# Weight slots of 4096 bytes, with the first two bytes of each row's piece left out of the load

## The chip, the core and the metric

The kernel runs on one core of one Trainium2 chip. The metric is the device time of one execution in microseconds; a kernel's time is the median over its runs.

## The reference

Pooled attention, whose output goes through a channel mix. Keys and values are averaged over 8 neighbouring positions, so that each of 576 queries sees 72 keys; the channel mix blends each token with the one before it, and then has a squared-ReLU layer and a sigmoid gate.

```python
# q, k, v: (8, 8, 576, 64)
k_p = k.reshape(B, H, Sp, pool, D).mean(axis=3)
v_p = v.reshape(B, H, Sp, pool, D).mean(axis=3)
scores = scale * np.matmul(q, k_p.transpose(0, 1, 3, 2))
attn = softmax(scores)
x = np.matmul(attn, v_p)            # then to (8, 576, 512)
# x_prev is x one token earlier
xk = mu_k * x + (1.0 - mu_k) * x_prev
xr = mu_r * x + (1.0 - mu_r) * x_prev
k = np.maximum(xk @ w_k, 0.0)       # w_k 512 x 1024
v = k * k @ w_v                     # w_v 1024 x 512
r = 1.0 / (1.0 + np.exp(-(xr @ w_r)))   # w_r 512 x 512
return r * v
```

The three weight arrays are float64, 10.5 MB together.

## The kernel before

The 4608 tokens are worked off in 12 chunks of 384. For each chunk the kernel computes scores, softmax, the attended values (`attended`), the blend with the token before (`shifted`), the hidden layer (`hidden`, matmuls at L1125), the gate (`gate`, L1178) and the output (`mixed`, L1211). The chunks from the second on multiply operands that are split into a high and a low part, three matmuls for one product; the first chunk (chunk 0) multiplies whole float32 operands.

The weights lie in HBM as float64, in 20 pieces of 128 rows by 512 doubles: `wk0` to `wk7`, `wr0` to `wr3`, `wv0` to `wv7`. A load (L589) moves one piece: 4096 bytes of each of 128 rows, 512 KB. A piece becomes float32 on the chip in `convert`: one cast (L621 on ScalarE, L624 on GpSimd or L627 on VectorE, by the table `TOP_BY`) takes the top two bytes of each double as a bf16 and writes them as the upper half of a float32 word in a scratch tile (its name in the profile is `turned`), and VectorE's L630 shifts the four bytes below them by 13 bits and joins the two. L630 writes over the front half of the same slot. `split` (L645 or L648, L656) later makes the high and low parts.

The lowest two bytes of a double take no part in this. The load before puts a row's 4096 bytes at byte 2 of its slot, so that the four bytes that L630 reads begin at a multiple of four:

```python
words = got[:, 1:2 * WP + 1].rearrange("p (n two) -> p n two", two=2)[:, :, 0]
first = got.bitcast(BF16)[:, 2:4 * WP + 2].rearrange("p (n four) -> p n four", four=4)[:, :, 2]
```

That leaves the slot 4224 bytes long (1056 int32), of which the last 126 are empty.

The order of the instructions of each engine is worked out by the program itself when it is built (class `Order`, with the table of due times `DUE`); each engine, and SyncE which issues nearly all DMAs (SPq in the profile), works its list off in that order. SyncE's first loads are written out by hand: "k0 k1 q1 wk1 q0 wk0 r0 q5 v0 q2 v1 wr2 v2 wr3 wk7 k2 q4 wv4 c0 wv6 q3 k3 wk3 wv1 wv2 wk5 wk2 wv7 wv3 v3 wr1 wr0 wk4 wv5 r1 wv0 wk6". A letter alone stands for keys, values, the values of the last keys, queries or constants (in the profile `in_kT`, `in_vm`, `in_vr`, `in_qT`, `in_mask` and `in_mu`). Some of these land in tiles that are used for something else later on: `early_sl`, `early_xrl`, `turned`. `summed` (L671) adds up keys and values over 8 positions with matmuls against an identity.

Of the kernel before, what the change touches and what calls it, by code (L numbers as in the profile page):

```python
# [10 lines left out]
I32 = mybir.dt.int32  # L11
BF16 = mybir.dt.bfloat16
F16 = mybir.dt.float16
U16 = mybir.dt.uint16
# [5 lines left out]
P = 128  # L20
# [11 lines left out]
WP = 512  # L32
# [315 lines left out]
def dve(n, lock=True):  # L348
    return "dve", 0.067 + n / 960, lock
# [15 lines left out]
def attention_then_channel_mix(  # L365
# [20 lines left out]
    sb = ctx.enter_context(tc.tile_pool(name="sb", bufs=1))  # L386
# [63 lines left out]
    for tag, n in (("sl", 2), ("xrl", 1), ("turned", 2)):  # L450
# [4 lines left out]
        for i in range(n):  # L455
            got = t[:, i]
# [93 lines left out]
    sources = {"k": w_k, "r": w_r, "v": w_v}  # L550
    held = {}

    def loads():

        for what in LOADS.split():
            kind, i = what[:-1] if what[0] == "w" else what[0], int(what.lstrip("ckvrqw"))
            yield from load(kind, i)
        done = set(LOADS.split())
        for i in range(NT):
            for b, s, *_ in tiles[i][2]:  # L560
                if first_tile[b] == i:
                    for what in (f"k{2 * b}", f"k{2 * b + 1}", f"v{2 * b}", f"v{2 * b + 1}", f"r{b}"):
                        if what not in done:
                            yield from load(what[0], int(what[1:]))
            if f"q{i}" not in done:
                yield from load("q", i)

    def load(kind, i):
        if kind == "c":
            yield "sp", 1.0, False  # L570
            nc.sync.dma_start(out=mask_sb, in_=mask)
            nc.sync.dma_start(out=mu_sb, in_=mu)
            order.fetched("mask", 100)
            order.fetched("mu", 100)
            return
        if kind == "q":
            qs = yield take("qs")
            yield "sp", 0.6, False
            nc.sync.dma_start(out=qs, in_=qT[i])
            held["q", i] = qs  # L580
            order.fetched(("q", i), 262)
            return
        if kind[0] == "w":
            slot = yield take("w")
            yield "sp", 0.6, False
            got = sb.tile([P, 2 * WP + 32], I32, name=f"got_{kind}{i}", tag=f"w{slot}")
            held["got", kind[1], i] = got
            held["slot", kind[1], i] = slot
            nc.sync.dma_start(  # L589
                out=got.bitcast(U16)[:, 1:1 + 4 * WP],  # L590
                in_=sources[kind[1]][:, i * WP:(i + 1) * WP].bitcast(U16),
            )
            order.fetched((kind, i), 512)
            return
        src, rows, cols = {
            "k": lambda: (kT[i // 2, :, 2 * (i % 2):2 * (i % 2) + 2, :], P, KEYS),
            "v": lambda: (vm[i // 2, :, 2 * (i % 2):2 * (i % 2) + 2, :], P, D),
            "r": lambda: (vr[i], 4 * KR, D),
        }[kind]()
        st = yield take("stage")  # L600
        yield "sp", 0.6, False
        v = st[:rows, :2 * POOL * cols].rearrange("p (g n) -> p g n", g=2)
        nc.sync.dma_start(out=v, in_=src)  # L603
        held[kind, i] = st, v
        order.fetched((kind, i), 2 * POOL * cols * rows / 256)

    def convert(kind, i):

        yield need(("w" + kind, i))
        got = held.pop(("got", kind, i))
        words = got[:, 1:2 * WP + 1].rearrange("p (n two) -> p n two", two=2)[:, :, 0]
        first = got.bitcast(BF16)[:, 2:4 * WP + 2].rearrange("p (n four) -> p n four", four=4)[:, :, 2]
        top = yield take("tmp")
        upper = top.bitcast(F16).rearrange("p (n two) -> p n two", two=2)[:, :, 1]
        by = TOP_BY[kind][i]
        if by == "a":
            yield "act", 0.62, False  # L620
            nc.scalar.copy(out=upper, in_=first)  # L621
        elif by == "g":
            yield "pool", 0.91, True
            nc.gpsimd.tensor_copy(out=upper, in_=first)  # L624
        else:
            yield "dve", 0.42, True
            nc.vector.tensor_copy(out=upper, in_=first)  # L627
        yield dve(WP)
        full[kind, i] = got[:, :WP].bitcast(F32)
        nc.vector.scalar_tensor_tensor(  # L630
            out=got[:, :WP], in0=words, scalar=13, in1=top.bitcast(I32),
            op0=ALU.logical_shift_right, op1=ALU.bitwise_or,
        )
        order.give("tmp", top)
        order.make(("full", kind, i))
# [605 lines left out]
    for b in range(B):  # L1241
        i = first_tile[b]
# [5 lines left out]
    for kind, n in (("k", NJT), ("r", NCT), ("v", NJT)):  # L1248
        for i in range(n):
            at = {"k": FIRST + 2.6 * i - 4, "r": FIRST + 20 + 2 * i - 3, "v": FIRST + 28 + 2.5 * i}[kind]  # L1250
            order.add(at, convert(kind, i))
            used = []
            if whole(0, kind):
                used = [("hid", 0, i, p) for p in range(len(PARTS))] if kind == "k" else [("gated" if kind == "r" else "mixed", 0)]
            at = {"k": 2.1 * i - 4, "r": 15 + i, "v": 25 + 0.8 * i}[kind]
            if not used:
                order.add({"k": FIRST + 2.6 * i - 3.5, "r": FIRST + 20 + 2 * i - 2.5, "v": FIRST + 28.5 + 2.5 * i}[kind], split(kind, i))
            else:
                order.add(later + at, split(kind, i, *used))
    for i in range(NT):  # L1260
# [11 lines left out]
        n = REST_BY[min(c, len(REST_BY) - 1)]  # L1272
# [73 lines left out]
```

## Time and profile before

| | |
|---|---|
| median of 3 runs | 600.98 us (600.29 to 601.49) |
| the profiled execution | 599.92 us |
| its span in the trace | 598.1 us |
| TensorE (PE) busy | 587.9 us, 98% of the span |
| VectorE (DVE) busy | 360.6 us, 60% |
| ScalarE (ACT) busy | 319.5 us, 53% |
| GpSimd (POOL) busy | 206.0 us, 34% |
| weight loads | 20, of 512 KB each, issued from 2.1 to 37.3 us |
| median us from issue to landing | wk 8.7, wr 9.3, wv 9.9 |

The profiled execution lasts 1.8 us longer than its span. A time from issue to landing holds the time that a load stands in the queues behind earlier ones, so it is long where many loads are in flight. The chain of waits in the profile goes back from the last instruction to what released it, and is what decides the time; busy time of an engine outside of it costs nothing.

### The profile page before, as it was taken

How to read it: one execution, taken by the hardware profiler on the slowest of the kernel's cores; microseconds unless marked ns; L12 is line 12 of the kernel's file. 1: busy time of each engine (PE TensorE's matmuls, PEld its weight loads, DVE VectorE, ACT ScalarE, POOL GpSimd, SP SyncE). 2: the span in 40 equal slices, each digit the busy share in tenths (PEclk: the TensorE clock that was granted, in tenths of full speed). 3: DMA queues.
4: the chain of work that ended last, by engine and by line, in shares of the span. 5: the costliest groups of instructions: out<-in, count | busy, mean ns of one | idle time of the engine just before them, and what ended most of it. 6: DMA issues, size and time to landing. Idle time of an engine off the chain costs nothing.

```text
span 598.1 us, 10517 instructions
## 1 busy us (share of the span) xinstructions
PE 587.9 (98%) x4026; PEld 491.4 (82%) x4026; DVE 360.6 (60%) x743; ACT 319.5 (53%) x657; POOL 206.0 (34%) x291
## 2 busy tenths in 40 slices
PE   7899999999999999999999999999999999999997
PEld 6766457978978988978978988987988988978985
DVE  5889978956967727657836726673954424423411
ACT  3577867657566463675555445555565335343420
POOL 1133276365126337147115309118416006005000
PEclk9999999999999999999999999999999999999999
DMA  8995075165364135335423115424014000001001
GB/s 322 405 380 188 39 191 172 43 173 204 115 179 114 45 80 175 121 104 151 168 57 77 59 37 157 133 93 115 19 61 94 19 1 35 19 0 37 19 0 53
DMA packets 43010, 66.61 MB, mean 111 GB/s; under 512 B 7504, under 2 KB 23120, under 8 KB 42960
## 3 DMA queue, kind: packets, MB, share of 16 engines
q1 hardware_dynamic: 42816, 65.82, 34.7%
q8 instruction: 31, 0.51, 0.3%
q14 instruction: 19, 0.16, 0.1%
q10 hardware_dynamic: 144, 0.13, 0.1%
HBM read 47.65 MB, written 18.28 MB: 110 GB/s over the span
## 4 chain that ended last, share of the span: by engine, by line
PE 94%; DMA 3%; ACT 1%; DVE 1%; SPq 1%; issue 0%; DVEq 0%; ACTq 0%
PE mm L1211 34%; PE mm L1125 33%; PE mm L1178 17%; PE pair L738 3%; PE pair L1037 3%; PE pair L1018 2%; DMA got_wk<-in_w_k 2%; DMA qs<-in_qT 1%; PE mm L671 1%; SPq L603 0%; SPq L589 0%; DVE stage L656 0%; ACT turned L621 0%; ACT ptr L970 0%; DVE ptr L973 0%
## 5 line engine op out<-in xcount | busy, mean ns | idle before, releaser
L1125 PE MATMUL mm<-xkh,w_k 128*128 128x384 f32 x704 | 180.7, 338 | 0.0
L1211 PE MATMUL mm<-w_v,sh 128*128 128x512 f32 x528 | 170.1, 396 | 0.0
L1125 PEld LDWEIGHTS mm<-xkh,w_k 128*128 128x128 f32 x704 | 127.4, 188 | 1.8 <-issue 0.5
L1211 PEld LDWEIGHTS mm<-w_v,sh 128*128 128x128 f32 x528 | 99.2, 188 | 27.2 <-issue 5.0
L1125 PE MATMUL mm<-xkl,w_k 128*128 128x384 f32 x352 | 118.4, 336 | 0.0
L1211 PE MATMUL mm<-w_v,sl 128*128 128x512 f32 x264 | 103.5, 392 | 0.0
L1079 DVE SCALAR_TENSOR_TENSOR xm<-pair,mu_sb,t 128x384 f32<-128x384 f32 x88 | 51.9, 614 | 85.3 <-POOL t L1070 44.2
L1178 PE MATMUL mm<-w_r,xrh 128*128 128x512 f32 x264 | 84.4, 394 | 0.0
L843 POOL TENSOR_TENSOR e<-e,sm 128x576 f32<-128x576 f32 x27 | 32.9, 1225 | 139.2 <-DVE sm L838 121.1
L1138 ACT ACTIVATE rk<-mm 128x384 f32<-128x384 f32 x88 | 43.1, 491 | 64.0 <-PE mm L1125 60.9
L1146 DVE SCALAR_TENSOR_TENSOR rk<-mm,rk 128x384 f32<-128x384 f32 x88 | 48.3, 552 | 32.4 <-ACT rk L1138 32.2
L1125 PEld LDWEIGHTS mm<-xkl,w_k 128*128 128x128 f32 x352 | 66.1, 188 | 0.0
L1059 ACT ACTIVATE t<-pair,om_sb 128x384 f32<-128x384 f32 x96 | 49.2, 579 | 29.6 <-PE pair L1037 28.4
L1097 POOL TENSOR_TENSOR xkl<-xm,xkh 128x384 fp32r<-128x384 f32 x44 | 47.0, 1072 | 46.6 <-ACT xkh L1095 46.5
L1153 ACT CAST sh<-rk 128x384 fp32r<-128x384 f32 x88 | 45.0, 513 | 32.3 <-DVE rk L1146 32.0
L656 DVE TENSOR_TENSOR sl<-rk,sh 128x384 fp32r<-128x384 f32 x88 | 50.6, 580 | 18.0 <-ACT sh L1153 17.2
L1178 PEld LDWEIGHTS mm<-w_r,xrh 128*128 128x128 f32 x264 | 49.7, 188 | 11.0
L1211 PEld LDWEIGHTS mm<-w_v,sl 128*128 128x128 f32 x264 | 49.6, 188 | 10.7
L1224 DVE TENSOR_TENSOR rs<-mm,rs 128x512 f32<-128x512 f32 (+1 forms) x37 | 24.8, 673 | 53.8 <-PE mm L1211 53.5
L1178 PE MATMUL mm<-w_r,xrl 128*128 128x512 f32 x132 | 52.1, 395 | 0.0
L1097 POOL TENSOR_TENSOR xrl<-xm,xrh 128x384 fp32r<-128x384 f32 x44 | 47.8, 1091 | 3.1 <-ACT xrh L1095 2.9
L656 POOL TENSOR_TENSOR stage<-stage 128x512 f32<-128x512 f32 (+5 forms) x51 | 44.6, 876 | 5.8 <-DMA stage<-in_vr 4.1
(108 smaller groups left out, 699.9 us busy)
## 6 DMA issues: line engine op xcount, KB each, us to landing
qs<-in_qT SPq DMA_DIRECT2D x36, 256.0 KB, 4.1
out<-rs SPq DMA_DIRECT2D x35, 256.0 KB, 2.0
passing<-pm SPq DMA_DIRECT2D x30, 288.0 KB, 2.1
stage<-in_kT SPq DMA_DIRECT2D x14, 576.0 KB, 4.8
turned<-passing SPq DMA_DIRECT2D x40, 192.0 KB, 3.9
stage<-in_vm SPq DMA_DIRECT2D x13, 512.0 KB, 3.9
got_wk<-in_w_k SPq DMA_DIRECT2D x8, 512.0 KB, 8.7
got_wv<-in_w_v SPq DMA_DIRECT2D x8, 512.0 KB, 9.9
```

Source lines behind the costliest of these rows:

```text
L656: (nc.vector if on_vector else nc.gpsimd).tensor_tensor(out=out, in0=a, in1=b, op=op)
L843: eng.tensor_tensor(out=e, in0=e, in1=sm.broadcast_to([P, 2, 4, KEYS]), op=ALU.mult)
L1059: nc.scalar.activation(out=t[:, m, 1:n + 1], in_=xp, func=AF.Copy, scale=om_sb[:, m, g:g + 1])
L1079: nc.vector.scalar_tensor_tensor(out=xm[:, :n], in0=xp, scalar=mu_sb[:, m, g:g + 1], in1=t[:, m, :n], op0=ALU.mult, op1=ALU.add,)
L1097: nc.gpsimd.tensor_tensor(out=lo, in0=xm[:, :n], in1=hi, op=ALU.subtract)
L1125: nc.tensor.matmul(out=hp, lhsT=w[:, o], rhs=x[:, ct, o_t], start=(ct == 0 and k == 0), stop=(ct == NCT - 1 and k == len(terms) - 1),)
L1138: nc.scalar.activation(out=rk[:, :n], in_=hp, func=AF.Relu)
L1146: nc.vector.scalar_tensor_tensor(out=rk[:, :n], in0=hp, scalar=0.0, in1=rk[:, :n], op0=ALU.max, op1=ALU.mult)
L1153: nc.scalar.copy(out=sh, in_=rk[:, :n])
L1178: nc.tensor.matmul(out=bank, lhsT=x[:, ct, o], rhs=w, start=(ct == 0 and k == 0), stop=(ct == NCT - 1 and k == len(terms) - 1),)
L1211: nc.tensor.matmul(out=bank, lhsT=s[:, o], rhs=w, start=(jt == 0 and k == 0), stop=(jt == NJT - 1 and k == len(terms) - 1),)
L1224: nc.vector.tensor_tensor(out=rs[:, o], in0=bank[:, o], in1=rs[:, o], op=ALU.mult)
```

## The change

The slot becomes 4096 bytes long. A load leaves out the first two bytes of each row's piece in HBM and lands the other 4094 at byte 0 of the slot. So every byte of a double stands two bytes lower than before, relative to byte 2, where it began: what was read at bytes 4 to 7 of the slot is now at bytes 0 to 3. The views `words` and `first` begin at the slot's byte 0 accordingly. The first double of each row lacks its lowest 16 bits, which nothing reads.

```diff
-            got = sb.tile([P, 2 * WP + 32], I32, name=f"got_{kind}{i}", tag=f"w{slot}")
+            got = sb.tile([P, 2 * WP], I32, name=f"got_{kind}{i}", tag=f"w{slot}")
...
             nc.sync.dma_start(
-                out=got.bitcast(U16)[:, 1:1 + 4 * WP],
-                in_=sources[kind[1]][:, i * WP:(i + 1) * WP].bitcast(U16),
+                out=got.bitcast(U16)[:, :4 * WP - 1],
+                in_=sources[kind[1]][:, i * WP:(i + 1) * WP].bitcast(U16)[:, 1:],
             )
...
-        words = got[:, 1:2 * WP + 1].rearrange("p (n two) -> p n two", two=2)[:, :, 0]
-        first = got.bitcast(BF16)[:, 2:4 * WP + 2].rearrange("p (n four) -> p n four", four=4)[:, :, 2]
+        words = got.rearrange("p (n two) -> p n two", two=2)[:, :, 0]
+        first = got.bitcast(BF16).rearrange("p (n four) -> p n four", four=4)[:, :, 2]
```

Nothing is moved in any engine's list: TensorE, VectorE, ScalarE and GpSimd have the same rows in the same order, with the same shapes. On SyncE only the weight loads differ, in the length of a row, counted in two-byte elements. This is its list from the second `v` load to the load of `wk3`:

```order
 L603 DMA early_sl<-in_vm 128x1024
-L589 DMA got_wr_198<-in_w_r 128x2048
+L589 DMA got_wr_198<-in_w_r 128x2047
 L603 DMA early_xrl<-in_vm 128x1024
-L589 DMA got_wr_217<-in_w_r 128x2048
-L589 DMA got_wk_222<-in_w_k 128x2048
+L589 DMA got_wr_217<-in_w_r 128x2047
+L589 DMA got_wk_222<-in_w_k 128x2047
 L603 DMA turned_99<-in_kT 128x1152
```

Each load stands where it stood, and a row remains one run of bytes. Since the slots become 128 bytes shorter, all tiles that lie behind the first slot in SBUF move to lower addresses, each by a multiple of 128 bytes.

## Rows read from the trace of the kernel before

**Rows 1.** The page, part 1: busy us of each engine.

```profile
PE 587.9 (98%) x4026; PEld 491.4 (82%) x4026; DVE 360.6 (60%) x743; ACT 319.5 (53%) x657; POOL 206.0 (34%) x291
```

**Rows 2.** The page, part 4: the chain's shares of the span by line.

```profile
PE mm L1211 34%; PE mm L1125 33%; PE mm L1178 17%; PE pair L738 3%; PE pair L1037 3%; PE pair L1018 2%; DMA got_wk<-in_w_k 2%; DMA qs<-in_qT 1%; PE mm L671 1%; SPq L603 0%; SPq L589 0%; DVE stage L656 0%; ACT turned L621 0%; ACT ptr L970 0%; DVE ptr L973 0%
```

**Rows 3.** The chain, over the whole span: two of its later pieces.

```profile
96.68 16.78 PE mm L1125 x96
...
508.82 16.75 PE mm L1125 x96
```

**Rows 4.** The chain in order of time, 0 to 82 us: start, us, what.

```profile
2.81 6.01 DMA qs<-in_qT
...
12.01 9.31 DMA got_wk<-in_w_k
...
21.39 0.78 ACT turned L621
...
25.25 0.68 ACT turned L621
...
26.59 1.25 PE mm L671 x8
...
34.34 6.75 PE mm L1125 x20
...
60.68 10.57 PE mm L1178 x24
```

**Rows 5.** ScalarE's timeline; in brackets idle time before and what ended it.

```profile
21.39 0.78 ACT L621 CAST turned<-got_wk 128x512 f16<-128x512 bf16 x1 [0.77 <-DMA got_wk<-in_w_k]
22.14 0.27 ACT L702 COPY vs<-mm 128x128 f32<-128x128 f32 x1
...
47.56 0.78 ACT L621 CAST turned<-got_wk 128x512 f16<-128x512 bf16 x1 [0.95 <-DMA got_wk<-in_w_k]
48.20 0.68 ACT L829 ACTIVATE e<-e 128x576 f32<-128x576 f32 x1
```

**Rows 6.** ScalarE's waits from 0 to 62 us: total, times, longest.

```profile
ACT turned L621 <- DMA got_wk<-in_w_k: 2.5, 4, 1.0
```

**Rows 7.** TensorE's timeline, the matmuls that the L702 above reads.

```profile
20.15 1.95 PE L671 MATMUL mm<-early_xrl,ident 128*128 128x128 f32 x16
```

**Rows 8.** DMA from 28 to 38 us, all engines of the core.

```profile
DMA packets 1112, 4.07 MB, mean 407 GB/s; under 512 B 124, under 2 KB 124, under 8 KB 1109
```

**Rows 9.** DMA from 3 to 4.5 us.

```profile
DMA packets 152, 0.63 MB, mean 418 GB/s; under 512 B 16, under 2 KB 16, under 8 KB 152
```

**Rows 10.** DMA issues around 11.06, 11.53 and 12.01 us: KB, us to landing.

```profile
early_xrl<-in_vm SPq DMA_DIRECT2D x1, 512.0 KB, 7.6
...
got_wr<-in_w_r SPq DMA_DIRECT2D x1, 512.0 KB, 8.4
...
got_wk<-in_w_k SPq DMA_DIRECT2D x1, 512.0 KB, 9.3
```

**Rows 11.** DMA from 358.5 to 361.5 us, by queue: packets, MB, share of 16 engines.

```profile
q1 hardware_dynamic: 1311, 0.63, 110.2%
```

**Rows 12.** Instructions on `got_wk`: duration in ns min/median/max, first and last start.

```profile
L630 DVE SCALAR_TENSOR_TENSOR got_wk<-got_wk,turned x8: 691/693/1056, 9.1 to 48.4; 128x512 int32<-128x512 int32 x8
L645 ACT CAST w_k<-got_wk x6: 604/618/621, 40.2 to 63.9; 128x512 fp32r<-128x512 f32 x6
L621 ACT CAST turned<-got_wk x5: 773/777/780, 21.4 to 47.6; 128x512 f16<-128x512 bf16 x5
```

**Rows 13.** The page, part 5: weight loads of TensorE, busy us, mean ns.

```profile
L1125 PEld LDWEIGHTS mm<-xkh,w_k 128*128 128x128 f32 x704 | 127.4, 188 | 1.8 <-issue 0.5
L1211 PEld LDWEIGHTS mm<-w_v,sh 128*128 128x128 f32 x528 | 99.2, 188 | 27.2 <-issue 5.0
L1178 PEld LDWEIGHTS mm<-w_r,xrh 128*128 128x128 f32 x264 | 49.7, 188 | 11.0
```

## Prediction

> **What bounds the kernel now.** I read the page first, then the chain of waits, then the DMA and the engines' timelines of the first 60 us, which is the only part where weight loads run. TensorE is busy for 98% of the span [rows 1], and the chain says the same by another route: nearly all of it is matmuls, and of DMA it holds the weight loads with 2% and the query loads with 1% [rows 2]. After some 60 us the chain runs from matmul group to matmul group, and the same group costs the same early and late: 96 hidden-layer matmuls take 16.78 us at 97 us and 16.75 us at 509 us [rows 3]. So a change of the weight loads can only matter ahead of that, and there the chain in order of time names the place [rows 4]: a query load that lands at 8.8 us (2.81 + 6.01), then the load of wk7, issued at 12.01 us and landed 9.31 us later, at 21.3 us; a cast of it on ScalarE at 21.39; from there other work of ScalarE up to 26.59 us, where TensorE takes over, and then TensorE almost without a break to the chunk's hidden layer (34.34) and, after a stretch of ScalarE and VectorE, to its gate (60.68).
>
> Why is a load of a weight that is needed last of its kind on the chain? ScalarE works its list in order. The cast of wk7 stands there idle for 0.77 us until the load lands, and behind it stands the copy L702 and all that leads to the matmuls of 26.59 us [rows 5]. The same holds for three more of its casts, 2.5 us of waiting in all, 1.0 us at the longest [rows 6]. So if the loads come later, ScalarE hands the delay on. If they come sooner, the gain is capped: L702 at 22.14 us reads matmuls that end at 22.10 us (20.15 + 1.95) and do not wait for wk7 [rows 5, 7].
>
> **The change, part by part.** It removes nothing, adds nothing, moves no instruction past another and adds no wait. What is left are four things whose price can change.
>
> *The rows' length.* 4094 bytes for 4096 is 0.05%. Over all 20 loads, at 1.3 us each (below), that is 0.01 us: nothing.
>
> *The rows' place.* A load has 128 rows on 16 engines, 8 rows for each. Now the landing is off by two bytes and the source is not; afterwards it is the other way round. What the first costs can be read. From 28 to 38 us nearly everything in flight is weight rows, and it moves at 407 GB/s [rows 8]: 4096 bytes at a sixteenth of that take 161 ns. From 3 to 4.5 us nearly all rows are key and query rows, with nothing shifted, at 418 GB/s [rows 9]: 157 ns for as many bytes. Consecutive landings say the same: the value load into early_xrl lands at 11.06 + 7.6 = 18.7 us, wr3 behind it at 11.53 + 8.4 = 19.9 and wk7 at 12.01 + 9.3 = 21.3, steps of 1.2 to 1.4 us [rows 10], thus 8 rows of 150 to 175 ns. So an unaligned landing costs between nothing and 4 ns a row. An unaligned source appears nowhere in this trace. Lower bound: the landing's 4 ns are saved and the source costs nothing, a gain of 4 ns a row. Upper bound: each row is broken so that a further short piece goes with it. The nearest row for a short piece is the fetch of the transposed probabilities, in 512-byte pieces: 110.2% of 16 engines over 3 us is 52.9 us for 1311 packets, 40 ns each [rows 11]. So the cost of a row changes by -4 to +40 ns. I take 0: one misplacement has been swapped for another, and the one that can be seen is all but free.
>
> What that is worth: up to and with wk7 there are five weight loads (wk1, wk0, wr2, wr3, wk7), 40 rows for each engine; with all 20 loads it is 160 rows. The lower bound gives wk7 0.16 us sooner, of which the cap of 22.10 us leaves less than 0.1, and at most 0.64 us if every wait profited in full. The upper bound makes wk7 1.6 us late, and the last load 6.4 us.
>
> A rule of the Trainium skill bears on this (DMA: Bandwidth & Descriptors, section "How a descriptor splits into AXI transactions"): a transfer that does not begin at a multiple of 256 bytes has its first transaction begin at the boundary below, and the bytes ahead are fetched for nothing but still take their time. The estimate by that page is that a row read from byte 2 to byte 4095 needs the same 16 transactions and 128 beats as one read from byte 0, so the sum by it is no change, where my upper bound would have 1.6 us and more. No run here shows an unaligned source, so I use it only to say that it speaks against the break-up of rows.
>
> *The casts and joins.* L621, L624, L627 and L630 read every fourth bf16 or every second int32, as before, from addresses four bytes lower. Such a cast takes 777 ns on ScalarE and the plain one of as many elements 618 [rows 12]: stepping costs 0.16 us, and nothing in the change alters the step. Bounds: it could gain those 0.16 us or lose as much, in each of the two casts on the chain [rows 4], thus 0.32 us either way. L630 takes 693 ns and lies on VectorE off the chain. I take 0.
>
> *Where everything else lies.* All tiles behind the first slot move by multiples of 128 bytes, and the steady state reads them. The 128 x 128 weight loads of TensorE take 188 ns on average, whether they read a weight slot (L1125), the squared hidden layer (L1211) or the gate's operand (L1178) [rows 13], so TensorE does not mind where its operand lies. Were this wrong, it would weigh: those three groups alone are 1496 loads, so 1 ns each would be 1.5 us. I take 0.
>
> Sum: 0 of 599.92 us, the profiled execution's own time (the span of 598.1 and the 1.8 us around it). That one ran 1.06 us under the median of the three runs shown, so against the median of 600.98 the forecast is 600.9, with the little that the landing may give back.
>
> **The rivals.**
>
> *Unaligned reads cost (slower).* Each row takes longer, and ScalarE, which waits for wk7, hands that on. For it speaks that no row here shows such a read, and that ScalarE's waits leave no slack at wk7. Against it, that an unaligned landing costs at most 4 ns. At 40 ns a row the time is 600.98 + 1.6 = 602.6 if only wk7's delay counts, and 607.4 if the last load's 6.4 us did in full; the truth would lie between, since wk6's cast at 47.56 us waits 0.95 us for its load already and more work stands behind it [rows 5], but many of the later weights are not used before the gate at 60.68 [rows 4]. It decides, that is, exceeds 0.2% or 1.2 us (about what a measurement of this kernel can tell from no change), from 30 ns a row if only wk7 counts, and from 7.5 ns a row if the lateness of the last load is passed on in full. Chance 14%.
>
> *The aligned landing frees the queues and the casts (faster).* 0.64 us from all rows and 0.32 us from the casts give 600.0, still inside 0.2%; to pass it, a row would have to gain 1.2/160 = 7.5 ns and every wait to profit. The cap at 22.10 us speaks against it. Chance 3%.
>
> *The new addresses change the steady state.* 1 ns on each of 1496 loads is 1.5 us, so 602.5 or 599.5. The even 188 ns and the even 16.75 us speak against it. Chance 3%, half of it either way.
>
> **How the numbers follow.** The forecast, no change that can be measured, has 80%. Faster gets 3% and half of the addresses' 3%, 5% when rounded up; slower 14% and the other half, 15%. The predicted time is that of the forecast, 600.9. The runs shown lie from 600.29 to 601.49, 0.6 us to each side. The forecast's own range is thus 600.0 to 601.6. The range given reaches below by the bounds of rows and casts, less than 0.96 us in all and part of it hidden, to 599.8, and above to the first part of the slower rival, 1.6 us for wk7 and a little of the runs' spread, 602.8.
>
> **What the profile afterwards would show.** If I am right, 28 to 38 us still moves 400 GB/s or more, wk7 lands 9.1 to 9.5 us after its issue, its cast stands idle for about 0.8 us, L621 still takes 777 ns, and the 96 hidden matmuls take 16.7 to 16.8 us. If reads cost, the rate from 28 to 38 us falls (161 ns a row becoming 200 would be 327 GB/s), the packets under 512 bytes may multiply, wk7 lands 10 us or more after its issue, and ScalarE's wait for weights grows far over 2.5 us. If addresses matter, the 188 ns or the 16.75 us move and the first 60 us do not. What would make me wrong is above all a cost of a source address off by two bytes that is larger than any row here lets one guess.

## The result and the profile after

The changed kernel takes 595.62 us (median of 6 runs, 594.43 to 597.05), the kernel before beside it 601.24 us: a ratio of 0.9901, 95% interval 0.9874 to 0.9927. The forecast was no change. The profiled execution took 595.48 us, its span 593.7.

The loads, casts and joins that the prediction had looked at in the first 60 us stayed as they were. The DMA rows of the changed kernel, first from 28 to 38 us, then from 3 to 4.5 us, then the issue of wk7 at 12 us with its time to landing:

```profile
DMA packets 1114, 4.06 MB, mean 406 GB/s; under 512 B 126, under 2 KB 126, under 8 KB 1112
...
DMA packets 153, 0.63 MB, mean 421 GB/s; under 512 B 16, under 2 KB 16, under 8 KB 153
...
got_wk<-in_w_k SPq DMA_DIRECT2D x1, 511.8 KB, 9.2
```

406 GB/s stand against 407 [rows 8], 421 against 418 [rows 9], 9.2 us against 9.3 [rows 10]. Joins and casts on `got_wk` are as long as before, too [rows 12]:

```profile
L630 DVE SCALAR_TENSOR_TENSOR got_wk<-got_wk,turned x8: 637/692/1624, 8.9 to 49.2; 128x512 int32<-128x512 int32 x8
L645 ACT CAST w_k<-got_wk x6: 602/618/624, 41.5 to 64.8; 128x512 fp32r<-128x512 f32 x6
L621 ACT CAST turned<-got_wk x5: 756/781/812, 21.2 to 47.3; 128x512 f16<-128x512 bf16 x5
```

ScalarE's waits for `wk` loads are 0.7 us in all, where [rows 6] has 2.5; but changed_again below, the same kernel, has 3.3, so that sum differs from one execution to the next and says nothing about the change.

The time went elsewhere. The chain of waits of the changed kernel in order of time (start, us, what), with the counterparts of [rows 3] and the last of [rows 4]:

```profile
26.45 2.29 PE mm L671 x8
...
61.66 10.57 PE mm L1178 x24
...
97.65 16.66 PE mm L1125 x96
...
505.35 16.66 PE mm L1125 x96
...
565.58 8.20 PE mm L1178 x36
573.78 16.33 PE mm L1211 x72
```

And the end of the same view of the kernel before, which the prediction had not shown:

```profile
569.62 8.34 PE mm L1178 x36
577.96 16.60 PE mm L1211 x72
```

Read it from the gate of chunk 0 (L1178 x24) to the end of the last matmuls. Before, these are 577.96 + 16.60 - 60.68 = 533.88 us, afterwards 573.78 + 16.33 - 61.66 = 528.45: a gain of 5.43 us. Up to that gate the profiled execution lost 0.98 us, which leaves the 4.4 us between the two spans. The gain has no place of its own: from the second chunk on, every group of matmuls of the hidden layer, the gate and the output is a little shorter. 36 gate matmuls go from 8.34 to 8.20 us, 72 output matmuls from 16.60 to 16.33, 96 hidden ones from 16.75 to 16.66; over 11 chunks (0.14 + 0.27 + 0.09) x 11 = 5.5 us. No instruction more or less, no wait that has gone: the same matmuls run at a closer pitch (the time from the start of one to the start of the next), 16.33/72 = 227 ns in place of 16.60/72 = 231. The gate of chunk 0, which multiplies whole float32 operands, has not moved: 10.57 us for 24 matmuls before [rows 4] and after.

The page's list of groups shows the same as means of the durations. Before, then the changed kernel:

```profile
L1211 PE MATMUL mm<-w_v,sh 128*128 128x512 f32 x528 | 170.1, 396 | 0.0
...
L1178 PE MATMUL mm<-w_r,xrh 128*128 128x512 f32 x264 | 84.4, 394 | 0.0
```

```profile
L1211 PE MATMUL mm<-w_v,sh 128*128 128x512 f32 x528 | 168.1, 392 | 0.0
...
L1211 PE MATMUL mm<-w_v,sl 128*128 128x512 f32 x264 | 102.9, 390 | 0.0
...
L1178 PE MATMUL mm<-w_r,xrh 128*128 128x512 f32 x264 | 83.3, 390 | 0.0
...
L1178 PEld LDWEIGHTS mm<-w_r,xrh 128*128 128x128 f32 x264 | 49.5, 188 | 10.1
```

The matmuls are 4 ns shorter; TensorE's weight loads read 188 ns, as in [rows 13].

The 0.98 us lost at the front are another matter. The windows of the changed kernel (length, busy us of each engine, granted clock, DMA share, GB/s) show TensorE's granted clock under 1 from 24 to 31 us, between its levels of 2.4 and 1.2 GHz on average over each stretch:

```profile
23.00:24.00 1.00, 0.23 (x1) 0.11 (x1) 0.95 (x5) 0.91 (x4) 0.93 (x1) 1.00 0.99 393
24.00:27.60 3.60, 2.24 (x14) 2.00 (x14) 2.87 (x8) 3.43 (x11) 0.11 (x1) 0.80 1.04 411
27.60:31.00 3.40, 3.40 (x47) 2.28 (x46) 1.84 (x4) 0.59 (x1) 0.77 (x1) 0.71 1.03 406
...
62.00:590.00 528.00, 528.00 (x3484) 450.10 (x3482) 312.23 (x642) 283.38 (x565) 189.63 (x262) 1.00 0.30 89
```

The kernel before, in the same view:

```profile
23.00:24.00 1.00, 0.22 (x3) 0.11 (x1) 0.96 (x4) 0.90 (x3) 0.80 (x1) 1.00 0.99 385
24.00:27.60 3.60, 2.24 (x17) 1.87 (x16) 2.96 (x8) 3.44 (x12) 0.24 (x1) 1.00 1.04 412
...
62.00:590.00 528.00, 528.00 (x3463) 447.73 (x3462) 310.79 (x641) 282.62 (x562) 188.72 (x261) 1.00 0.30 89
```

While the clock was down, 8 matmuls at L671 took 2.29 us where they took 1.25 [rows 4]. Why it fell is open: TensorE had been busy for 0.23 us of the microsecond before 24 us, but for 0.22 us in the kernel before as well, where the clock stayed at 1.00. The mean granted clock differs between executions of either kernel (0.991 to 1.000 for the kernel before, 0.996 to 1.000 for the changed one), and the experiment old_load_4352 below, at a clock of 1.000, has its gate at 60.97 us. So the loss is not put down to the change. From 62 us on the clock is 1.00 in both, so it has no part in the gain either.

### The profile page after: what moved, and what is told of

Read it like the earlier page. It is cut to its first block, busy times and chain, and to the rows that moved or that the text cites. A ratio compares the mean times of both kernels' runs of the same rounds, so it can differ in the third digit from the quotient of the medians.

```text
span 593.7 us, 10517 instructions
## 1 busy us (share of the span) xinstructions
PE 583.1 (98%) x4026; PEld 490.9 (83%) x4026; DVE 362.0 (61%) x743; ACT 319.1 (54%) x657; POOL 206.2 (35%) x291
## 4 chain that ended last, share of the span: by engine, by line
PE 93%; DVE 3%; ACT 2%; DMA 1%; issue 1%; SPq 0%; POOL 0%; DVEq 0%; ACTq 0%; POOLq 0%
PE mm L1211 34%; PE mm L1125 32%; PE mm L1178 17%; PE pair L1037 3%; PE pair L738 3%; PE mm L671 2%; PE pair L1018 2%; DMA got_wk<-in_w_k 1%; DVE got_wk L630 0%; DVE mx L809 0%; ACT e L816 0%; DVE stage L656 0%; DVE w_k L656 0%; DVE sm L831 0%; DVE ptr L973 0%
## 5 line engine op out<-in xcount | busy, mean ns | idle before, releaser
L1211 PE MATMUL mm<-w_v,sh 128*128 128x512 f32 x528 | 168.1, 392 | 0.0
L1211 PEld LDWEIGHTS mm<-w_v,sh 128*128 128x128 f32 x528 | 99.1, 188 | 25.7 <-issue 5.0
L1211 PE MATMUL mm<-w_v,sl 128*128 128x512 f32 x264 | 102.9, 390 | 0.0
L1178 PE MATMUL mm<-w_r,xrh 128*128 128x512 f32 x264 | 83.3, 390 | 0.0
L1178 PEld LDWEIGHTS mm<-w_r,xrh 128*128 128x128 f32 x264 | 49.5, 188 | 10.1
L1211 PEld LDWEIGHTS mm<-w_v,sl 128*128 128x128 f32 x264 | 49.6, 188 | 9.9
L1178 PE MATMUL mm<-w_r,xrl 128*128 128x512 f32 x132 | 51.5, 390 | 0.0
```

Of the source, the lines that this page charges most:

```text
L1178: nc.tensor.matmul(out=bank, lhsT=x[:, ct, o], rhs=w, start=(ct == 0 and k == 0), stop=(ct == NCT - 1 and k == len(terms) - 1),)
L1211: nc.tensor.matmul(out=bank, lhsT=s[:, o], rhs=w, start=(jt == 0 and k == 0), stop=(jt == NJT - 1 and k == len(terms) - 1),)
```

## The experiments

**The theories.** What moves with the slot's length is the place of all tiles behind the first slot. A slot of 4224 bytes is 8 x 512 + 128 long; every other tile that the large matmuls read (x, the squared layer, their low parts) is a multiple of 512 bytes long. So before, each slot lay 128 bytes further off the others' grid than the slot ahead of it, which is 0 and 128 by turns modulo 256; with 4096 bytes all lie on the grid. (These distances, here and below, are worked out from the lengths in the code; the traces hold no addresses.) TensorE reads two things at a time, the moving operand of one matmul and the weights of the next: in the changed kernel a gate matmul starts at 565.41 us, the weight load for the one behind it at 565.42. Theory *places*: the distance between these two, in the low bits of the address, sets the pitch. Rivals: the *loads* that land at byte 0; the *absolute place* of a weight row; the *even steps* from one slot to the next.

**slots_4224: the slot's length alone undone.** The new loads stay.

```diff
-            got = sb.tile([P, 2 * WP], I32, name=f"got_{kind}{i}", tag=f"w{slot}")
+            got = sb.tile([P, 2 * WP + 32], I32, name=f"got_{kind}{i}", tag=f"w{slot}")[:, :2 * WP]
```

> The changed kernel with only the slot's length put back: 4224 bytes, while the loads still bring 4094 bytes to byte 0. Theory places (the gain comes from where the weight slots lie against the other operands that TensorE reads, since every slot now begins a multiple of 512 bytes from the next): the gain is gone, 600 to 602 us, 96 hidden matmuls in 16.75 us, 36 gate matmuls in 8.34 us, 72 output matmuls in 16.6 us. Theory loads (the gain comes from rows that land at byte 0): it stays, 594 to 597 us.

600.85 us against 600.04 for the kernel before, ratio 1.0006 (0.9986 to 1.0026). The chain's end is that of the kernel before to the hundredth:

```profile
571.58 8.34 PE mm L1178 x36
579.93 16.60 PE mm L1211 x72
```

The gain is gone while the loads are there. The loads bring nothing that shows.

**old_load_4352: the slot's length alone changed, another way.** The kernel before, its loads untouched, with slots of 17 x 256 bytes.

```diff
-            got = sb.tile([P, 2 * WP + 32], I32, name=f"got_{kind}{i}", tag=f"w{slot}")
+            got = sb.tile([P, 2 * WP + 64], I32, name=f"got_{kind}{i}", tag=f"w{slot}")
```

> The kernel before with its loads as they were (4096 bytes to byte 2), and a slot of 4352 bytes in place of 4224, so that slots begin 17 times 256 bytes apart: a multiple of 256, not of 512. Theory places, if what counts is the place modulo 256: the whole gain without the new loads, 594 to 597 us. If it is modulo 512: some of it or nothing, 597 to 602 us. Theory loads: no gain, 600 to 602 us.

595.16 us, ratio 0.9916 (0.9895 to 0.9937): the whole gain, with a longer slot and a load at byte 2. The groups are those of the changed kernel:

```profile
564.87 8.20 PE mm L1178 x36
573.07 16.33 PE mm L1211 x72
```

So it is not that slots got shorter either, but that their distance became a multiple of 256.

**slots_apart_128 and all_shifted_128: relation or absolute place.** The first puts unused tiles round the weight slots, which then all lie 128 bytes off the others (the last slot stands apart from the rest and gets a pair of its own); the second puts one ahead of all of them together.

```diff
+            if kind == "xkh" and c == 0:
+                sb.tile([P, 96], F32, name="pad1", tag="pad1")
+            if kind == "xkl" and c == 1:
+                sb.tile([P, 96], F32, name="pad3", tag="pad3")
...
+            if slot == 0:
+                sb.tile([P, 32], F32, name="pad0", tag="pad0")
             got = sb.tile([P, 2 * WP], I32, name=f"got_{kind}{i}", tag=f"w{slot}")
...
+        if slot == WSLOTS - 1:
+            sb.tile([P, 32], F32, name="pad2", tag="pad2")
```

```diff
+    sb.tile([P, 32], F32, name="pad", tag="pad")
     early = {}
```

> The changed kernel with unused tiles of 128 and 384 bytes ahead of and behind the weight slots, so that all weight slots lie 128 bytes off the 512-byte grid of the other operands, each slot by as much. Theory places, as a relation between the two operands that TensorE reads at a time: slow in the steady state, gate matmuls 8.3 us or more for 36, 600 us or more. Theory even steps (only the change of place from one slot to the next costs): still fast, 594 to 597 us.

> The changed kernel with one unused tile of 128 bytes ahead of all operands that TensorE reads from the second chunk on, so that all of them move by 128 bytes together. Theory places as a relation: still fast, 594 to 597 us. Theory absolute place (a weight row must begin at 192 modulo 256, wherever the other operand lies): slow, 599 us or more.

Apart: 603.79 us, ratio 1.0070 (1.0044 to 1.0095), slower than the kernel before, although the steps from slot to slot are even. Its chain:

```profile
559.07 16.90 PE mm L1133 x96
...
575.97 8.40 PE mm L1186 x36
584.37 16.82 PE mm L1219 x72
```

Shifted together: 595.32 us, ratio 0.9915 (0.9894 to 0.9935):

```profile
548.00 16.66 PE mm L1126 x96
564.66 8.20 PE mm L1179 x36
572.87 16.33 PE mm L1212 x72
```

That rules out the absolute place and the even steps; what counts is the relation. (Padding moves the line numbers: the hidden layer is L1133 or L1126 here, the gate L1186 or L1179, the output L1219 or L1212.) The gate of chunk 0 takes 10.57 us in both, so the whole float32 matmuls show no such price.

**slots_apart_256, slots_apart_64 and slots_apart_192: which distance.** The same edit with tiles of 256 and 256, 64 and 448, 192 and 320 bytes.

```diff
-                sb.tile([P, 32], F32, name="pad0", tag="pad0")
+                sb.tile([P, 64], F32, name="pad0", tag="pad0")
...
```

> The changed kernel with unused tiles of 256 bytes ahead of and behind the weight slots: every slot 256 bytes off the 512-byte grid of the other operands. Theory modulo 256 (two operands that TensorE reads at a time are free of each other when they begin a multiple of 256 bytes apart): as fast as the changed kernel, 594 to 597 us, 36 gate matmuls in 8.20 us. Theory modulo 512: slow, 600 us or more, gate matmuls 8.3 us or more.

> The changed kernel with unused tiles of 64 and 448 bytes ahead of and behind the weight slots: every slot 64 bytes off the grid. Theory modulo 256: slow like 128 bytes off, 600 to 606 us, gate matmuls 8.3 us or more. Theory modulo 64 with another cause for the 128 bytes: fast, 594 to 597 us.

> The changed kernel with unused tiles of 192 and 320 bytes ahead of and behind the weight slots. Theory modulo 256, with a price that grows to the middle: like 64 bytes off, 36 gate matmuls in 8.24 us, 69 output matmuls in 16.0 us, 595 to 598 us. Theory that the price grows with the distance itself: as slow as 128 bytes off or slower, gate matmuls 8.40 us or more.

256 bytes off: 594.79 us, ratio 0.9907 (0.9889 to 0.9924), as fast as on the grid. 64 off: 596.22 us, ratio 0.9935 (0.9910 to 0.9959), which by the time alone cannot be told from the changed kernel; the groups can:

```profile
505.64 16.64 PE mm L1133 x96
...
549.38 16.77 PE mm L1133 x96
566.15 8.24 PE mm L1186 x36
574.39 16.50 PE mm L1219 x72
```

The gate loses 0.04 us and the output 0.17, a fifth and a third of what 128 bytes cost them (0.20 and 0.49). So neither expectation holds: it is not slow like 128, and it is not free. 192 off, a single execution: 600.94 us. Its groups split up:

```profile
553.75 16.64 PE mm L1133 x96
570.39 8.39 PE mm L1186 x36
578.78 16.81 PE mm L1219 x72
```

Gate and output are as slow as at 128, the hidden layer is as fast as on the grid. The first expectation fails; the second comes close in the gate (8.39 for 8.40 or more) and fails in the hidden layer. In gate and output the weight slot is the moving operand, in the hidden layer it is what is loaded as weights, so a distance of 192 for the one is one of -192, that is 64 modulo 256, for the other. In gate and output the price is thus not the same 64 bytes ahead of a multiple of 256 as 64 behind it. It does not simply go by the signed distance of moving operand from weights either: in slots_apart_64 the hidden layer has 192 in that sense, and takes 16.64 to 16.77 us, not the 16.90 of 128.

**only_sl_apart_128: one operand of one line.** If it is the relation of two operands, moving one of them must touch its own matmuls alone.

```diff
+            pad = {"sl": 32, "xrl": 96}[tag]
+            sb.tile([P, pad], F32, name=f"pad_{tag}", tag=f"pad_{tag}")
             t = sb.tile([P, n, 2 * POOL * KEYS], F32, name=f"early_{tag}", tag=tag)
```

> The changed kernel with unused tiles of 128 and 384 bytes ahead of and behind the tile of the low half of the squared hidden layer (sl) alone, which TensorE loads as weights for one in three of the output's matmuls. Theory relation of the two reads: only the output's matmuls get longer, 69 of them 15.9 to 16.2 us in place of 15.87 (less than with all operands apart, 16.23, since two loads in three are on the grid), while gate (8.20 for 36) and hidden (16.66 for 96) stay; the time 596 to 598.5 us. Theory of a chance effect of the whole layout: all three lines move, or none.

598.30 us, ratio 0.9963 (0.9951 to 0.9975), as the theory of a relation expected. Only the output's groups move, 69 matmuls to 16.15 and 72 to 16.65 us; gate and hidden layer stay at 8.20 and 16.66. The page's groups show which of the output's matmuls (line numbers are up by two):

```profile
L1127 PE MATMUL mm<-xkh,w_k 128*128 128x384 f32 x704 | 179.8, 336 | 0.0
L1213 PE MATMUL mm<-w_v,sh 128*128 128x512 f32 x528 | 169.6, 395 | 0.0
...
L1213 PE MATMUL mm<-w_v,sl 128*128 128x512 f32 x264 | 104.7, 397 | 0.0
L1180 PE MATMUL mm<-w_r,xrh 128*128 128x512 f32 x264 | 83.3, 390 | 0.0
```

Those with sl rise from 390 to 397 ns, and those with sh, whose own weights have not moved, from 392 to 395: half of these run ahead of one with sl. The starts of the records in this trace tell them apart: from a matmul with sh to the next with sh it is 227 ns (median), as on the grid; from sh to sl 232; from sl to sh 234, where the changed kernel has 227 for all three. So the price falls on the matmul ahead of sl, during which sl is loaded, and on that with sl itself. The first is what theory places says; the second it does not explain.

**all_on_grid and changed_again: is there more to be had?** The tiles `turned`, and all behind them, moved by 64 bytes, so that the attention's operands are on the grid with their partners as well.

```diff
+    const.tile([P, 16], F32, name="pad")
     turned_sb = [const.tile([P, CH // BLOCK, 6 * BLOCK], F32, name=f"turned{i}") for i in range(2)]
```

> The changed kernel with an unused tile of 64 bytes ahead of the tiles turned, so that these, and all behind them, begin at multiples of 256 bytes, as the small tiles vs, vbd_r and ks0 that TensorE reads beside them already do. Theory modulo 256, extended to the attention's matmuls (L1018, 4 in 0.70 us, L1037, 16 in 1.45 us, L738, 96 in 1.66 us): these get up to 2% shorter, at most 1 us over 11 chunks, so 593.5 to 595.5 us. Theory that those matmuls are limited by something else: the same as the changed kernel, 594.5 to 596 us, with 0.70, 1.45 and 1.66 us as they are.

> The changed kernel as it is, beside the one with all tiles on the grid: 594 to 597 us by every theory.

594.82 us, ratio 0.9907 (0.9894 to 0.9921), beside 595.57 us, ratio 0.9916 (0.9902 to 0.9931), for the changed kernel on the same chip: the intervals overlap. The attention's groups keep 0.70, 1.45 and 1.66 us. Whether something else limits them is not shown: at 64 bytes the gate lost 0.04 of 8.20 us, and a share as small would be under 0.01 us in each of these groups. No version here beats the changed kernel by what can be measured.

All in one table; the first column is the distance of the weight slots from the other operand, modulo 256, in gate and output (in the hidden layer, with the roles exchanged, 64 and 192 change places); the ratio is to the kernel before, run beside it; the last three are us of the chain's groups (output: 72 matmuls).

| | distance | ratio to before | gate, 36 | output, 72 | hidden, 96 |
|---|---|---|---|---|---|
| before | 0 or 128, by slot | 1 | 8.34 | 16.60 | 16.75 |
| slots_4224 | 0 or 128, by slot | 1.0006 | 8.34 | 16.60 | 16.75 |
| changed | 0 | 0.9901 | 8.20 | 16.33 | 16.66 |
| old_load_4352 | 0 | 0.9916 | 8.20 | 16.33 | 16.66 |
| all_shifted_128 | 0 | 0.9915 | 8.20 | 16.33 | 16.66 |
| slots_apart_256 | 0 | 0.9907 | 8.20 | 16.33 | 16.66 |
| slots_apart_64 | 64 | 0.9935 | 8.24 | 16.50 | 16.64 to 16.77 |
| slots_apart_128 | 128 | 1.0070 | 8.40 | 16.82 | 16.90 |
| slots_apart_192 | 192 | one execution, 600.94 us | 8.39 | 16.81 | 16.64 |
| only_sl_apart_128 | 0, sl 128 | 0.9963 | 8.20 | 16.65 | 16.66 |

## Why the prediction was wrong

*The rows' length and place: right.* An unaligned source costs nothing that can be seen: 406 GB/s, wk7 landed after 9.2 us, and slots_4224, with the new loads alone, has a ratio of 1.0006 (0.9986 to 1.0026) to the kernel before. The slower rival had 14% and is out.

*The casts and joins: right.* L621 takes 781 ns and L630 692. The cap at the first cast held as well: ScalarE still waits 0.71 us for wk7 (0.77 before), and its copy L702 behind that starts at 22.01 us (22.14 before), so the profile shows no gain there beyond the 0.1 us that the prediction allowed.

*Where everything else lies: here it failed.* The step took "0", because "TensorE does not mind where its operand lies", on two grounds. The first was that TensorE's weight loads take 188 ns whatever they read. That is so, before and after, and in slots_apart_128 too, where all is slow, so it is no witness: what is longer is the matmul beside the load, by some 4 ns in the kernel before against the changed one. The page before had that row, 396 ns for L1211 with sh, and nothing to compare it with but 392 with sl. The second ground, given with the rival, was that 96 hidden matmuls take as long early as late. But each chunk reads the same tiles at the same places; evenness over time says nothing about a price that is paid in every chunk. The term was priced per instruction on the wrong ones as well: 1496 weight loads at 1 ns, where 2244 matmuls (704 + 352 + 528 + 264 + 264 + 132) gained 5.43 us, 2.4 ns each. The rival "the new addresses change the steady state" named the right place, with 3%, half of that for the wrong sign, and 599.5 us where 595.62 was measured.

*What would have made it visible:* the lengths in the code. A slot of 8 x 512 + 128 bytes amid tiles of multiples of 512 puts every other slot 128 bytes, modulo 256, off its partner, and the change makes it 0 for all. No row of the page says that this could matter. But the trace of before holds matmuls at both distances. A gate tile is 12 matmuls, always against the same slots, and comes 33 times; by the starts of the records, the median time from one to the next lies between 226 and 240 ns, depending on its place among the 12, and at 226 or 227 for all in the changed kernel. Equal matmuls whose pitch goes by the slot that they read are a sign that the place matters, and the means of 394 and 188 ns hide it.

*Shown and not shown.* Shown is that the pitch goes by the distance of the two operands that TensorE reads, that 256 bytes are as good as 0, and that it is not the loads, the slot's length, the absolute place or the steps. That the two reads get in each other's way in the memory is a reading that fits most of it, but it was argued, not measured; it leaves open why a matmul with sl gets longer itself. How the price runs between 0 and 256 bytes is open too: 64 costs little and 128 and 192 much in gate and output, while in the hidden layer only 128 costs its full price. The Trainium skill (SBUF — State Buffer, section "Who interferes with whom") gives TensorE two independent read ports, one for the moving operand and one for weights. If "independent" is taken to mean that the place of one operand against the other is free, these runs differ: 231 against 227 ns a matmul by it.

## What to carry to other kernels

Where TensorE is the bound, as here, where it was worth 1%, let the tiles that it reads at the same time, moving operand and weights, begin a multiple of 256 bytes apart. A pad of 32 words in a tile that has 21 copies shifts each copy against its partners; round the tile's length, not only its use. A mean over many matmuls can hide two kinds of them: look at the times from start to start one by one. And before a term is set to nothing because "the address does not matter", look for two rows that differ in the address and in nothing else.

## What the runs showed of the hardware that had not been expected

TensorE's pitch for a 512-column matmul of split operands (float32r) depends on where its two operands lie: 16.33/72 = 227 ns at distances of 0 and 256 bytes, 16.50/72 = 229 at 64, 16.82/72 = 234 at 128, 16.81/72 = 233 at 192. For 384 columns it is 16.66/96 = 173.5 ns on the grid and 16.90/96 = 176 at 128. The whole float32 matmuls of chunk 0's gate do not show it: 10.57/24 = 440 ns in every run, at 128 as on the grid. A source address off by two bytes in a 4094-byte row cost nothing: 406 GB/s against 407.
